# Twelve of the fourteen tiles that hold split weights made 64 bytes longer

## The chip, the cores and the metric

One core of a Trainium2 chip. The metric is the device time of one execution in microseconds (us).

## The reference

Top-32 attention over 4 batches, 8 heads, 576 positions and 64 columns a head, then two gated feed-forward layers (512 to 1536 to 512) over the 2304 tokens.

```python
scores = scale * np.matmul(q, k.transpose(0, 1, 3, 2))
kth = np.partition(scores, -top_k, axis=-1)[..., -top_k:-top_k + 1]
scores = np.where(scores >= kth, scores, -1000000000.0)
attn = np.exp(scores - np.max(scores, axis=-1, keepdims=True))
attn = attn / (np.sum(attn, axis=-1, keepdims=True) + 1e-09)
x = np.matmul(attn, v)                      # heads side by side: [2304, 512]
g = x @ w_gate
x = (g * (1.0 / (1.0 + np.exp(-g))) * (x @ w_val)) @ w_out        # moe
gate = 1.0 / (1.0 + np.exp(-(x @ w_gate2)))
return (gate * (x @ w_val2)) @ w_out2                             # moe2
```

## The kernel before

The 2304 tokens are cut into five chunks of 256, 512, 512, 512 and 512 tokens (`SIZES`, in units of 64). For each chunk `attention` makes the scores on TensorE, finds the 32nd largest of each row on VectorE (`top_full`, L888 and L890), normalizes and multiplies with v (`pv`, L977); then `moe` runs both feed-forward layers (L1018). The order of all instructions on all engines is written out beforehand by a planner (`Plan.run`), from durations that stand in the source. It knows nothing of addresses in the on-chip memory (SBUF), so the order is the same for any placement of the tiles.

Chunk 0 (mode "N") multiplies in plain fp32: `decode` unpacks a slab of 512 weight columns into a tile `wf` (GpSimd and ScalarE, L540 to L573), a DMA copies it to DRAM (`sw`, L576), and TensorE uses the tile at once as the stationary operand. The 72 tiles of chunk 0 go round a ring of 24 places: 12 in `home_pool` (`home0` to `home11`) and 12 in a pool of their own (`xf12` to `xf23`). So the first layer's gate and value slabs use home0 to home11 and then xf12 to xf23, its output slabs (input `hn`) home0 to home11, and the second layer's output slabs xf12 to xf23.

Chunks 1 to 4 (mode "P") split each operand into a high and a low part that are both fp32r. `slab` loads a slab again from DRAM into `raw`; `split_ops` makes the high part w[0] by a copy (ScalarE or GpSimd, L520 or L522) and the low part w[1] by a subtraction on GpSimd (L525). Seven pairs of tiles are used in turn (`w_tiles`): the pairs (home0, home1) to (home10, home11), and (wu0, wu1) in the pool `arena`. For one output tile, `mms` issues 12 matmuls of 128x512: four with w[0] and the inputs' high part, four with w[1] and the high part, four with w[0] and the low part. Inputs are `xh` and `xl` (pool `xs`), and `hh` and `hl`. Each matmul is preceded by its own weight load (LDWEIGHTS), which runs while the matmul before it streams its input. The scores of chunks 2 to 4 are fp32r too (`stacked_scores`, L678): stationary `qs`, inputs `kh` and `kl`, 288 columns.

Where the tiles lie follows from the order of the pools and the sizes of their tiles. In bytes from the start of a partition, before the change:

| tiles | start | bytes each |
|---|---|---|
| home0 to home11 (w[0], w[1] of six pairs; wf) | 17024 | 2048 |
| arena: wr0, wr1, wu0, wr2, wu1, wu2 | 41600 | 4096 or 2048 |
| a tile of 64 bytes, then xh, xl | 60096, 68288 | 8192 |
| eight (128 bytes), a tile of 64 bytes, x32, ... | 76480 | |
| hh, hl of chunks 1 to 4 | 159424, 184000 | 24576 |
| in chunk 0: xn0, xn1, hn | 159424, 163520, 167616 | 4096, 12288 |
| in chunk 0: xf12 to xf23 | 198336 | 2048 |
| qs | 212672 | 4096 |
| kh0, kh1, kl0, kl1 | 219072, 221376, 223680, 225984 | 2304 |

A slab's four blocks of 128x128 lie 512 bytes apart in its tile, the four inputs that meet them 2048 bytes apart (1024 in chunk 0). In this document the *lead* of a weight load is the address that it starts at, less the address at which the input of the matmul then running starts, modulo 512; with steps of 512, 1024 and 2048 it is the same for all blocks of a tile.

Of the kernel before, what the change touches and what calls it, by code (L numbers as in the profile page):

```python
# [19 lines left out]
P = 128  # L20
# [94 lines left out]
class Ring:  # L115
    def __init__(self, make, bufs):
        self.make, self.bufs, self.gens, self.next, self.after = make, bufs, [], 0, []
        self.before = lambda i: []
# [4 lines left out]

    def last(self, slot):
        return [g for g in self.gens if g.i % self.bufs == slot][-1:]


class Gen:
# [5 lines left out]
    def __getitem__(self, k):  # L134
        return self.tile[k]
# [212 lines left out]
def attn_moe_kernel(ctx: ExitStack, tc, qT, kT, qD, kD, vL, wall, outT):  # L348
# [6 lines left out]
    def pool(name, bufs, space=None):  # L355
        kw = {"space": space} if space is not None else {}
        return ctx.enter_context(tc.tile_pool(name=name, bufs=bufs, **kw))
# [19 lines left out]
    def phase_pool(n, name, bufs):  # L377
        if phases["now"] != n:
            if phases["stack"] is not None:
                phases["stack"].close()  # L380
            phases["now"], phases["stack"], phases["pools"] = n, ExitStack(), {}
            for nm, b in phase_rings[n]:
                phases["pools"][nm] = phases["stack"].enter_context(tc.tile_pool(name=f"{nm}{n}", bufs=b))
        return phases["pools"][name]
# [7 lines left out]
    home_pool = pool("home", 1)  # L392
# [9 lines left out]
    def home(nm, dtype=F32):  # L402
        i = int(nm.split("_")[1]) % (WF + XF if dtype == F32 else WF)
        if i >= WF:
            return phase_pool(0, "xf", XF).tile([P, 512], dtype, tag=f"xf{i}", name=nm, bufs=1)
        return home_pool.tile([P, 512], dtype, tag=f"home{i}", name=nm, bufs=1)
    R = {
        "x32": ring("x32", [P, NPAIR, TP], F32, 1),
        "sil": ring("sil", [P, HW], F32, SIL),
# [22 lines left out]
    kinds = [{"N": 0}.get(m, 1) for m in MODES]  # L432
    PHASE = [sorted(set(kinds)).index(k) for k in kinds]
    R["wf", 0] = Ring(home, WF + XF)
    phase_rings = {}
    for n in sorted(set(PHASE)):
# [3 lines left out]
        if "N" in kinds:  # L440
            T = max(SIZES[c] for c in mine if MODES[c] == "N") * 64
            specs.update(xn=([P, ND, T], F32, 2), hn=([P, NF, T], F32, 1), q=([P, S], F32, Q_RING),
                         k=([P, S], F32, K_RING))
# [35 lines left out]
    def w_tiles(nm):  # L479
        out = []  # L480
        for k in range(2):
            kind, i = w_home[2 * (int(nm.split("_")[1]) % WH) + k]
            out.append(home(f"w_{i}_{nm}", F32R) if kind == "wf" else
                       arena.tile([P, 512], F32R, tag=f"wu{i}", name=f"w_{i}_{nm}", bufs=1))
        return out
# [345 lines left out]
    def row_tile(sg, stg, a, e, pg):  # L831
        eg = new("e")

        def src():
            return sg[:, e].rearrange("p a b -> p (a b)")
        last, m0 = top_full(sg, src, stg, a)

        def base(eng):
# [26 lines left out]
        def norm(eng):  # L865
# [3 lines left out]
            else:  # L869
                nc.gpsimd.tensor_scalar(o, o, stg[:, 35:36], 1.0, op0=ALU.mult, op1=ALU.mult)  # L870
        x = op("act", act(S), drop, deps=[last], uses=[sg, stg], allocs=[eg], prio=P_EX[now[0]], table="exp")
        y = op(BASE, 0, base, deps=[last, m0], uses=[stg])
        y = op("act", 765, ex, deps=[x, y], uses=[eg, stg], allocs=[pg], prio=P_EX[now[0]], table="exp")
        y = op(EPS, 0, eps, deps=[y], uses=[stg])
# [122 lines left out]
    def moe(c):  # L997
# [16 lines left out]
        def mms(pg, blk, src, n, first, last):  # L1014
            i = 0
            for a, x in terms:
                for d in range(4):
                    nc.tensor.matmul(pg[:, :n], blk(a, d), src(x, d), start=first and i == 0,  # L1018
                                     stop=last and i == 4 * len(terms) - 1)
                    i += 1  # L1020
# [180 lines left out]
```

## Time and profile before

| | us |
|---|---|
| median of 3 runs | 1221.41 (1220.84 to 1222.0) |
| the profiled execution | 1221.71 |
| its span, first to last instruction | 1219.9 |

| engine | busy us | share of the span |
|---|---|---|
| TensorE, matmuls (PE) | 1165.9 | 96% |
| TensorE, weight loads (PEld) | 905.5 | 74% |
| GpSimd (POOL) | 945.3 | 77% |
| VectorE (DVE) | 868.8 | 71% |
| ScalarE (ACT) | 855.7 | 70% |

A matmul's record covers its way through the array, so records of neighbours overlap; how often matmuls follow each other is read from their starts. "L1018" is a line of the kernel before. The granted clock of TensorE is given as a share of 2.4 GHz.

### The profile page before, as it was taken

The page shows a single profiled execution, that of the slowest core. Times are in us where ns is not written, and L with a number is a line of the kernel's source. Part 1 is how long each engine was busy: PE and PEld are TensorE (multiplying, and loading weights), DVE is VectorE, ACT ScalarE, POOL GpSimd, SP SyncE. Part 2 cuts the span into 40 slices and gives each one's busy share as a digit, 9 for nine tenths or more (in the row PEclk, how much of TensorE's full clock was granted, in tenths as well). Part 3 has the DMA queues.
Part 4 walks back from the last instruction along what each step waited for, and adds up shares of the span by engine and source line. Part 5 has one row for each costly group of instructions (what it writes and reads, how often), then busy time and mean ns, then how long its engine had stood idle before and what let it go on. Part 6 is the DMA issues. An engine that isn't in the chain of part 4 may idle for free. (4 is left out here: it accounts for less than half of the span.)

```text
span 1219.9 us, 18873 instructions
## 1 busy us (share of the span) xinstructions
PE 1165.9 (96%) x6148; PEld 905.5 (74%) x6148; DVE 868.8 (71%) x1852; ACT 855.7 (70%) x1756; POOL 945.3 (77%) x954
## 2 busy tenths in 40 slices
PE   4698999998999999999899999999999999999998
PEld 1377866775777777878688787788777888888886
DVE  7999999999999999849498999999911101211110
ACT  6898999999886878858677978888733433432441
POOL 5677889896899798978777898879956786765761
PEclk9899999999999999999899999999999999999999
DMA  8787888883787886866647687667773333232320
GB/s 272 244 297 235 270 283 268 263 275 119 187 248 206 227 223 186 224 210 180 170 115 213 173 270 195 203 175 222 202 211 87 96 112 119 89 104 87 104 87 35
DMA packets 175170, 228.22 MB, mean 187 GB/s; under 512 B 112352, under 2 KB 117728, under 8 KB 175072
## 3 DMA queue, kind: packets, MB, share of 16 engines
q1 hardware_dynamic: 175072, 227.02, 62.6%
q8 instruction: 48, 0.79, 0.3%
q14 instruction: 50, 0.41, 0.1%
HBM read 149.13 MB, written 51.90 MB: 165 GB/s over the span
## 5 line engine op out<-in xcount | busy, mean ns | idle before, releaser
L525 POOL TENSOR_TENSOR w_w<-raw,w_w 128x512 fp32r<-128x512 f32 x288 | 374.7, 1307 | 116.6 <-ACT w_w L520 110.8
L1018 PE MATMUL ps_m<-xh,w_w 128*128 128x512 f32 x1536 | 385.0, 393 | 1.1 <-POOL xh L522 1.1
L1018 PEld LDWEIGHTS ps_m<-xh,w_w 128*128 128x128 f32 x1536 | 284.2, 188 | 61.3 <-POOL xh L522 1.5
L888 DVE MAX8 st<-wk 128x8 f32<-128x576 f32 x432 | 312.9, 745 | 0.4
L520 ACT ACTIVATE w_w<-raw 128x512 fp32r<-128x512 f32 x214 | 132.9, 624 | 124.1 <-PE ps_m L1018 71.0
L890 DVE MATCH_REPLACE8 wk<-st,wk 128x576 f32<-128x576 f32 x288 | 212.8, 740 | 0.0
L1018 PE MATMUL ps_m<-xl,w_w 128*128 128x512 f32 x768 | 207.3, 392 | 0.0
L1018 PE MATMUL ps_m<-hh,w_w 128*128 128x512 f32 x768 | 192.2, 392 | 0.0
L1018 PEld LDWEIGHTS ps_m<-xl,w_w 128*128 128x128 f32 x768 | 144.3, 188 | 31.7
L1018 PEld LDWEIGHTS ps_m<-hh,w_w 128*128 128x128 f32 x768 | 142.8, 188 | 30.8 <-issue 0.7
L525 POOL TENSOR_TENSOR hl<-h,hh 128x512 fp32r<-128x512 f32 x96 | 125.5, 1307 | 3.4 <-ACT hh L520 2.0
L888 DVE MAX8 st<-s 128x8 f32<-128x576 f32 x144 | 106.3, 745 | 24.8 <-ACT s L705 15.1
L848 ACT ACTIVATE e<-s,st 128x576 f32<-128x576 f32 x144 | 110.5, 769 | 15.9 <-DVE st L888 15.7
L989 DVE SCALAR_TENSOR_TENSOR h<-sil,ps_m 128x512 f32<-128x512 f32 x48 | 32.6, 680 | 117.1 <-PE ps_m L1018 117.1
L852 ACT ACTIVATE p<-e,st 128x576 f32<-128x576 f32 x144 | 110.7, 769 | 3.9 <-POOL pl L956 1.4
L1053 ACT ACTIVATE sil<-ps_m 128x512 f32<-128x512 f32 (+2 forms) x132 | 67.6, 512 | 58.1 <-PE ps_m L1018 57.8
L890 DVE MATCH_REPLACE8 wk<-st,s 128x576 f32<-128x576 f32 x144 | 106.5, 740 | 0.0
L1018 PE MATMUL ps_m<-hl,w_w 128*128 128x512 f32 x384 | 103.6, 392 | 0.0
L1018 PE MATMUL ps_m<-xn,wf 128*128 128x128 f32 (+1 forms) x576 | 93.9, 313 | 2.7 <-ACT xn L983 1.9
L977 PE MATMUL ps_v<-pt,v 128*64 128x128 f32 (+6 forms) x800 | 92.7, 377 | 0.2 <-ACT pt L936 0.2
L1018 PEld LDWEIGHTS ps_m<-xn,wf 128*128 128x128 f32 x576 | 80.3, 191 | 14.9 <-issue 3.9
L989 DVE SCALAR_TENSOR_TENSOR sil<-sil,ps_m 128x512 f32<-128x512 f32 (+1 forms) x72 | 39.0, 542 | 69.6 <-ACT sil L1053 69.6
(69 smaller groups left out, 1690.7 us busy)
## 6 DMA issues: line engine op xcount, KB each, us to landing
raw<-sw SPq DMA_DIRECT2D x144, 512.0 KB, 3.7
wr<-in_wall_dram SPq DMA_DIRECT2D x72, 512.0 KB, 4.7
sp_pl<-pl SPq DMA_DIRECT2D x44, 576.0 KB, 3.7
sw<-wf SPq DMA_DIRECT2D x72, 256.0 KB, 3.0
v<-in_vL_dram SPq DMA_DIRECT2D x34, 320.0 KB, 3.9
kr<-in_kD_dram SPq DMA_DIRECT2D x34, 288.0 KB, 3.1
k<-in_kT_dram SPq DMA_DIRECT2D x16, 288.0 KB, 4.5
out_dram<-h SPq DMA_DIRECT2D x16, 256.0 KB, 2.4
```

Of the source, the lines that this page charges most:

```text
L520: nc.scalar.activation(out=hi(), in_=raw(), func=AF.Copy)
L525: (nc.gpsimd if eng == "pool" else nc.vector).tensor_sub(lo(), (lo_raw or raw)(), lo_hi() if lo_hi else f32(hi()))
L848: nc.scalar.activation(out=eg[:], in_=src(), func=AF.Prelu, bias=stg[:, 31:32], scale=-1.0, alpha=1.0 / STEEP)
L852: nc.scalar.activation(out=pg[:, e * S:(e + 1) * S], in_=eg[:], func=AF.Exp, bias=stg[:, 32:33], scale=-STEEP, accum_out=stg[:, 33:34])
L888: nc.vector.max(out=stg[:, 4 * k:4 * k + 8], in_=src() if k == 0 else fresh[:])
L890: nc.vector.match_replace(out=fresh[:], in_to_replace=stg[:, 4 * k - 4:4 * k + 4], in_values=src() if k == 1 else fresh[:], imm_value=NEG)
L977: nc.tensor.matmul(og[64 * h:64 * h + 64, :W], vg[:, 8 + h if i == 4 else 4 * h + i], ptg[:, 4 if i == 4 else 5 * h + i, :W], start=(i == ...
L989: nc.vector.scalar_tensor_tensor(out=out, in0=t, scalar=1.0, in1=x, op0=ALU.add, op1=ALU.mult)
L1018: nc.tensor.matmul(pg[:, :n], blk(a, d), src(x, d), start=first and i == 0, stop=last and i == 4 * len(terms) - 1)
L1053: nc.scalar.activation(out=sg[:, :n], in_=pg[:, :n], func=AF.Tanh, scale=0.5)
```

## The change

Each of the twelve tiles in `home_pool` is asked for with 528 columns instead of 512, so it takes 2112 bytes instead of 2048. A small class `Front` hands out the first 512 columns of it, whatever is asked for. The two tiles wu0 and wu1 and the twelve tiles xf12 to xf23 stay as they are.

```diff
+class Front:
+    def __init__(self, t):
+        self.t, self.shape = t, [P, 512]
+
+    def __getitem__(self, k):
+        return self.t[:, :512]
+
...
         if i >= WF:
             return phase_pool(0, "xf", XF).tile([P, 512], dtype, tag=f"xf{i}", name=nm, bufs=1)
-        return home_pool.tile([P, 512], dtype, tag=f"home{i}", name=nm, bufs=1)
+        return Front(home_pool.tile([P, 528], dtype, tag=f"home{i}", name=nm, bufs=1))
```

Tile home(i) then starts at 17024 + 2112 i, and all tiles behind the home pool start 12 x 64 = 768 bytes later.

## Rows read from the trace of the kernel before

**Rows 1.** The chain that ended last, its shares by line

```profile
by line: PE ps_m L1018 33.2%; DVE st L888 4.5%; DVE wk L890 3.8%; PE ps_v L977 1.3%; PE ps_s L678 0.6%; DVE h L989 0.5%; issue 0.4%; ACT p L852 0.2%; POOL w_w L525 0.2%; ACT w_w L520 0.1%; ACT p L868 0.1%; DVE st L863 0.1%; ACT e L848 0.1%;
```

**Rows 2.** The same chain from 860 us: start us, us, what

```profile
899.70 16.69 PE ps_m L1018 x72
916.38 2.31 PE ps_v L977 x20
918.69 297.15 PE ps_m L1018 x1296
1215.85 0.03 ACTq L1124
1215.87 0.04 issue
1215.92 0.60 ACT h L1124
```

**Rows 3.** Stretches: busy us (instructions) of each engine, granted clock, DMA share, GB/s

```profile
400.00:500.00 100.00, 98.96 (x494) 78.53 (x493) 99.08 (x213) 82.20 (x163) 87.25 (x89) 1.00 0.81 214
700.00:800.00 100.00, 98.93 (x492) 77.42 (x492) 99.25 (x217) 83.20 (x170) 85.45 (x88) 1.00 0.75 220
800.00:905.00 105.00, 105.00 (x521) 82.94 (x520) 88.40 (x189) 76.92 (x142) 90.64 (x97) 1.00 0.74 207
918.69:1215.84 297.15, 297.14 (x1297) 243.17 (x1296) 35.77 (x52) 104.78 (x175) 190.38 (x155) 1.00 0.30 92
```

**Rows 4.** Instructions of L1018: duration ns min/median/max, first and last start

```profile
L1018 PEld LDWEIGHTS ps_m<-xh,w_w x1536: 186/188/192, 295.4 to 1181.3; 128*128 128x128 f32 x192
L1018 PE MATMUL ps_m<-xh,w_w x1536: 387/392/505, 295.4 to 1181.6; 128*128 128x512 f32 x192
...
L1018 PEld LDWEIGHTS ps_m<-hl,w_w x384: 187/188/189, 379.5 to 1215.2; 128*128 128x128 f32 x192
L1018 PE MATMUL ps_m<-hl,w_w x384: 388/392/398, 379.7 to 1215.4; 128*128 128x512 f32 x192
...
L1018 PE MATMUL ps_m<-hn,wf x192: 379/379/483, 140.9 to 279.0; 128*128 128x256 f32 x192
```

**Rows 5.** Order of time on PE, 818 to 827 us: start us, us, instructions

```profile
819.42 0.29 PE L678 MATMUL ps_s<-kh,qs 128*128 128x288 f32 x1
819.55 0.29 PE L678 MATMUL ps_s<-kl,qs 128*128 128x288 f32 x1
819.68 0.29 PE L678 MATMUL ps_s<-kh,qs 128*128 128x288 f32 x1
819.81 0.30 PE L678 MATMUL ps_s<-kl,qs 128*128 128x288 f32 x1
819.95 2.00 PE L1018 MATMUL ps_m<-xh,w_w 128*128 128x512 f32 x8
...
825.46 0.30 PE L678 MATMUL ps_s<-kh,qs 128*128 128x288 f32 x1
825.59 0.29 PE L678 MATMUL ps_s<-kl,qs 128*128 128x288 f32 x1
825.73 0.29 PE L678 MATMUL ps_s<-kh,qs 128*128 128x288 f32 x1
825.86 0.30 PE L678 MATMUL ps_s<-kl,qs 128*128 128x288 f32 x1
825.99 1.31 PE L1018 MATMUL ps_m<-xh,w_w 128*128 128x512 f32 x5
```

**Rows 6.** Instructions of L678, duration ns min/median/max, first and last start

```profile
L678 PEld LDWEIGHTS ps_s<-kh,qs x176: 186/188/192, 305.0 to 858.6; 128*128 128x128 f32 x176
L678 PEld LDWEIGHTS ps_s<-kl,qs x176: 186/188/192, 305.2 to 858.7; 128*128 128x128 f32 x176
```

**Rows 7.** Order of time on PE in chunk 0, around 146 and 259 us

```profile
145.82 5.34 PE L1018 MATMUL ps_m<-hn,wf 128*128 128x256 f32 x24
...
258.74 1.89 PE L1018 MATMUL ps_m<-hn,wf 128*128 128x256 f32 x8
```

**Rows 8.** Instructions on other engines that touch weight tiles: duration ns min/median/max

```profile
L525 POOL TENSOR_TENSOR w_w<-raw,w_w x288: 1266/1302/1812, 268.6 to 1197.3; 128x512 fp32r<-128x512 f32 x144
L525 POOL TENSOR_TENSOR hl<-h,hh x96: 1272/1302/1820, 307.3 to 1184.9; 128x512 fp32r<-128x512 f32 x96
L520 ACT ACTIVATE w_w<-raw x214: 612/624/635, 265.9 to 1196.6; 128x512 fp32r<-128x512 f32 x107
L520 ACT ACTIVATE hh<-h x82: 614/632/637, 312.4 to 1183.7; 128x512 fp32r<-128x512 f32 x82
L573 POOL TENSOR_TENSOR wf<-wf,wu x45: 1263/1277/1287, 12.8 to 266.1; 128x512 int32<-128x512 int32 x45
```

**Rows 9.** Stores of wf: DMA issues of 60 to 85, then 85 to 110 us

```profile
sw<-wf SPq DMA_DIRECT2D x6, 256.0 KB, 2.3
...
sw<-wf SPq DMA_DIRECT2D x5, 256.0 KB, 2.9
```

## The prediction

> **What bounds the kernel now.** I read the chain that ended last first. A third of the span on it is the feed-forward matmul, L1018, and some 8% the search for the 32nd largest score on VectorE [rows 1]. Its last link says most: from 918.69 us on, 1296 matmuls of L1018 follow each other without a gap, and 0.7 us behind them the kernel ends [rows 2]. Next, the stretches [rows 3]: in the last one PE is busy for 297.14 of 297.15 us, while ACT has 104.78 and POOL 190.38. In the three stretches shown between 400 and 905 us PE is busy for 98.9 to 100% and DVE for 84 to 99%, so there both set the pace. The granted clock is 1.00 in all four stretches, the level of 2.4 GHz, so no clock is to be won.
>
> So one number carries the case: how often an fp32r matmul of 512 columns starts. 297.15 us / 1296 = 229.3 ns. L1018 issues 3456 of them (1536 + 768 + 768 + 384, over the four inputs; [rows 4] has the first and the last group). A change of 1 ns in that number is worth 3456 x 1 ns = 3.5 us where PE is the limit throughout. What I have to judge is whether it hangs on where the weights lie relative to the input that streams while they are loaded.
>
> **The change part by part.** *What moves.* No instruction, semaphore or transfer is added, removed or reordered; the planner doesn't see addresses. Before, every split weight tile starts at 128 modulo 512, and xh, xl, hh and hl at 192, so every weight load of L1018 in chunks 1 to 4 has lead 448. After, the inputs move by 768 bytes, that is 256 modulo 512, and home(i) by 64 i: its lead becomes 448 - 256 + 64 i = 192 + 64 i modulo 512. The high parts (even i) get 192, 320, 448, 64, 192, 320, the low parts (odd i) 256, 384, 0, 128, 256, 384; the pair in wu0 and wu1 stays at 448. A high part serves 8 of 12 matmuls. So 5/7 x 2/3 + 6/7 x 1/3 = 16/21 of the matmuls, 2633 of 3456, get a new lead.
>
> *What a new lead costs a matmul.* The trace of before has no L1018 load in fp32r at another lead, but its nearest relatives have. (1) The score matmuls L678 are fp32r with 288 columns, and their groups of four come in two patterns. With the addresses of qs, kh and kl, the group at 819.42 has leads 256, 256, 0 and, where its last matmul runs beside the load of the next split weight, 448. The group at 825.46 has 128, 128, 384 and 320. From the first start to the start of the L1018 matmul behind them both take 0.53 us, 132.5 ns a matmul [rows 5]. So six of the eight multiples of 64 stand in these two groups, and 448, the lead of today, costs there what the five others do. (2) The weight load itself takes 186 to 192 ns, median 188, under all these leads: in L1018 at 448 [rows 4] and in L678 at the others [rows 6]. (3) In chunk 0, plain fp32, the first layer's hn matmuls take their weights from home tiles (lead 448) and the second layer's from xf tiles (lead 0). 24 of the one take 5.34 us, 8 of the other 1.89 us [rows 7]. Less the 0.379 us of the last one's own record [rows 4], that is 4.961 / 23 = 215.7 ns and 1.511 / 7 = 215.9 ns from start to start. No difference either; the home tiles' new leads in chunk 0 cost nothing by it.
>
> I take 0 for the term. Its bounds: the rows of (1) are given to 0.01 us, so a difference of up to 0.01 us over four matmuls, 2.5 ns each, could hide in one pair of groups; over some fifty such groups I allow 1.5 ns either way. 2633 x 1.5 ns = 3.9 us, in either direction, as a gain can't be excluded.
>
> *Other engines.* GpSimd's subtraction for the low part reads raw and w[0] and writes w[1]; before, all lie at the same place modulo 512. The same operation for hl has its three tiles at 384, 192 and 192, and the median of both is 1302 ns [rows 8]: 0. ScalarE's copy takes 624 ns for w[0] and 632 for hh [rows 8], so bounds of 0 and 8 ns x 214 copies = 1.7 us; I take 0 on the end, because PE hides it: in the last stretch ACT is idle for 192 us of 297 [rows 3]. If that cover were gone, it would cost at most those 1.7 us. In chunk 0, L573 writes home and xf tiles, at 128 and at 192 modulo 512, within 1263 to 1287 ns for all 45 [rows 8]: 0. The stores of wf land 2.3 us after issue in the stretch with home tiles and 2.9 us in that with xf tiles [rows 9], bounds of -0.6 and +0.6 us a store; what they wrote is loaded again only in chunk 1, so nothing waits for them: 0. If loads did wait for the last stores, it would be one such delay, 0.6 us.
>
> *The sum.* The profiled execution took 1221.71 us: 1219.9 of span and 1.8 around it. It lies 0.3 us above the median of 1221.41. All terms are 0, so the span stays 1219.9, the profiled execution 1221.7 and the median 1221.4.
>
> *A rule against this.* The trace shows 229.3 ns from start to start [rows 2]. The Trainium skill, in "TensorE: Matmul & The Clock Gate", section "Wait — 56ns, not 53.3ns?", gives back-to-back matmuls as the columns divided by 2.4 GHz plus about 2.5 ns, which would be 215.7 ns here; that is an estimate from the page, and the trace doesn't agree, it is 13.6 ns slower. The same page, section "Step-by-step: what each phase is for", says that TensorE reads moving operand and weights through two independent ports, so that a load takes no bandwidth from the running matmul. By that the 13.6 ns aren't a clash of the two reads, and no placement wins them back; the equal spacing in [rows 5] agrees.
>
> **The rivals.** *Faster: the distance above the plain rate is a clash that lead 448 has and others haven't.* The nearest row for an undisturbed rate is chunk 0's 215.7 ns for a pass over 256 columns of fp32 [rows 7], if an fp32r pass takes 512 columns in that time; then 229.3 - 215.7 = 13.6 ns are the clash. Freed for all 2633 matmuls: 2633 x 13.6 ns = 36 us, to about 1185; freed for half of them, about 1203. That is the most, since DVE sets the pace too before 905 us [rows 3]. For it: all matmuls of L1018 in fp32r share one lead today, so the trace can't show them without a clash. The plain rate on the Trainium skill's page "TensorE: Matmul & The Clock Gate" would give the same time. Against it: 448 and five other leads cost the same in the groups of four [rows 5]. Chance 0.08.
>
> *Slower: a clash at leads 64 or 192.* These two are nowhere in the trace with a load beside a matmul of L1018 or L678. They fall on home6 (64), home0 and home8 (192), three of seven high parts: 3/7 x 2/3 = 2/7 of the matmuls, 987. If a clash cost as much as the 13.6 ns above, that is 13.4 us, 1234.8 us. It passes 0.2% (2.44 us) from 2.5 ns a matmul. For it: nothing measured at these two. Against: the six others are alike, and 320 and 448 are odd multiples of 64 as well. Chance 0.08.
>
> *The change doesn't do what it says.* Should the pool round tiles up to multiples of 512 bytes, leads would not spread and the time would be that of before, 1221.4. The same time as the forecast, so no chance of its own is taken from it.
>
> **How the numbers follow.** Forecast 1221.4 us, no change that can be measured: 0.84 including the bounds of 3.9 us. A measurement of this kernel can tell about 0.2%, 2.4 us, from no change, and part of the bounds lies beyond that: I give 0.02 of the 0.84 to faster and 0.02 to slower. ScalarE's possible 1.7 us adds 0.01 to slower. With 0.08 for each rival: faster 0.10, same 0.79, slower 0.11. Range: 1221.4 - 3.9 = 1217.5 below; above, 3.9 + 1.7 us, 1227.0. It leaves out nearly all of the two rivals, 0.16.
>
> **What would show it.** The 1296 matmuls at the end should again take 297 us (229.3 ns each). With the rivals: down to 284 us (16/21 of 1296 x 13.6 ns = 13.4 us less), or up to 302 us (2/7 of 1296 x 13.6 ns = 5.0 us more), and then with a pattern by tile: slower runs of matmuls with home0, home6 and home8, and as fast as before with wu0. The weight loads' median should stay 188 ns, GpSimd's subtraction 1302 ns. I would be wrong if fp32r loads beside 512 columns behave otherwise than beside 288, if the address modulo 512 isn't what matters, or if the 768 bytes by which everything else moves touch a tile that was well placed by absolute address.

## The result, and the profile after

| | before | after |
|---|---|---|
| median of 18 runs each, us | 1221.25 (1217.43 to 1223.62) | 1227.76 (1222.63 to 1232.09) |
| profiled execution, us | 1221.71 | 1224.54 |
| its span, us | 1219.9 | 1222.7 |

The ratio is 1.0056, 95% interval 1.0045 to 1.0068: slower by 0.56%, 6.5 us between the medians. The forecast of no measurable change was wrong, and 1227.76 lies above its range. All lines of the kernel behind the new class stand 8 lines further down: L1018 is now L1026, L678 is L686, L525 is L533.

The end of the chain that ended last, after the change (start us, us, what):

```profile
914.38 2.31 PE ps_v L985 x20
916.69 301.96 PE ps_m L1026 x1296
1218.66 0.03 ACTq L1132
1218.68 0.04 issue
1218.73 0.60 ACT h L1132
```

The 1296 matmuls that took 297.15 us [rows 2] take 301.96 us, 233.0 ns each and not 229.3. That is 4.81 us in one stretch, with nothing else in the chain. The stretches of after (busy us and instructions of PE, weight loads, DVE, ACT and POOL, granted clock, DMA share, GB/s):

```profile
600.00:700.00 100.00, 99.14 (x506) 78.14 (x504) 88.01 (x183) 79.08 (x169) 78.21 (x81) 1.00 0.63 176
700.00:800.00 100.00, 99.36 (x494) 77.38 (x493) 99.90 (x222) 80.58 (x166) 84.17 (x87) 1.00 0.74 217
916.69:1218.65 301.96, 301.95 (x1297) 243.82 (x1296) 35.78 (x52) 104.80 (x175) 189.85 (x155) 1.00 0.29 90
```

In the last stretch the clock is 1.00, the level of 2.4 GHz, as before; ACT and POOL have as much work as before [rows 3], and as much idle time. So neither the clock nor a late weight tile explains it. The order of time on PE, inside that stretch, after the change:

```profile
1000.49 2.02 PE L1026 MATMUL ps_m<-hh,w_w 128*128 128x512 f32 x8
1002.35 1.10 PE L1026 MATMUL ps_m<-hl,w_w 128*128 128x512 f32 x4
1003.28 2.02 PE L1026 MATMUL ps_m<-hh,w_w 128*128 128x512 f32 x8
```

and before it:

```profile
1001.14 1.99 PE L1018 MATMUL ps_m<-hh,w_w 128*128 128x512 f32 x8
1002.98 1.08 PE L1018 MATMUL ps_m<-hl,w_w 128*128 128x512 f32 x4
1003.89 1.99 PE L1018 MATMUL ps_m<-hh,w_w 128*128 128x512 f32 x8
```

A group of twelve takes 2.79 us from start to start (1000.49 to 1003.28), where it took 2.75. No instruction and no wait lies between; the same matmuls simply follow each other more slowly. The weight loads' records don't tell: they are as long as before [rows 4].

```profile
L1026 PEld LDWEIGHTS ps_m<-xh,w_w x1536: 186/188/192, 294.9 to 1183.6; 128*128 128x128 f32 x192
L1026 PE MATMUL ps_m<-xh,w_w x1536: 387/394/505, 294.9 to 1183.8; 128*128 128x512 f32 x192
```

The matmuls' records are 394 ns in the median, up from 392. From the starts of the single matmuls between 295 and 905 us, the mean step between two of L1018 with nothing else between them (steps over 300 ns, which hold waits, left out) is 229.5 ns before and 231.4 ns after. For the 2160 matmuls ahead of the last 1296 that is up to 4.1 us more, less what DVE's own pace hides there. With the end's 4.8 us it makes 8.9 us; the medians differ by 6.5.

The two profiled executions differ by less, 2.8 us. One reason can be the clock. Between 599 and 605.5 us the granted clock of before was 0.50, 1.2 GHz, behind 3 us in which PE was busy for 0.82 us; after has 1.00 in that place. First two rows before the change, then one after:

```profile
596.00:599.00 3.00, 0.82 (x4) 0.35 (x2) 0.17 (x1) 2.98 (x10) 1.22 (x2) 0.96 0.39 147
...
599.00:605.50 6.50, 5.54 (x17) 2.34 (x19) 0.69 (x1) 1.90 (x4) 5.35 (x5) 0.50 0.41 126
```

```profile
599.00:605.50 6.50, 5.83 (x32) 2.98 (x33) 0.69 (x1) 2.73 (x6) 5.13 (x4) 1.00 0.47 147
```

That is 17 PE instructions against 32 in the same 6.5 us, so the dip costs about half of its length, some 3 us (an estimate). Such dips differ from trace to trace: that of the kernel with lead 0, below, has two of them, near 284 and 601 us, that of lead 320 one, near 285 us. The last 1296 matmuls have none in any trace, so the experiments are read from them first.

### The profile page after: what moved, and what is told of

Same layout as the page of the kernel before. It is cut to its first block, busy times and chain, and to the rows that moved or that the text cites. A ratio compares the mean times of both kernels' runs of the same rounds, so it can differ in the third digit from the quotient of the medians.

```text
span 1222.7 us, 18873 instructions
## 1 busy us (share of the span) xinstructions
PE 1172.1 (96%) x6148; PEld 906.5 (74%) x6148; DVE 869.7 (71%) x1852; ACT 856.0 (70%) x1756; POOL 945.3 (77%) x954
## 4 chain that ended last, share of the span: by engine, by line
PE 62%; DVE 24%; ACT 7%; POOL 3%; issue 2%; DMA 2%; SPq 0%; POOLq 0%; ACTq 0%; DVEq 0%
PE ps_m L1026 54%; DVE st L896 11%; DVE wk L898 9%; PE ps_v L985 4%; PE ps_s L686 3%; ACT p L860 1%; ACT wu L562 1%; ACT e L856 1%; DVE wf L578 1%; DMA wr<-in_wall_dram 1%; ACT pt L944 1%; PE ps_s L703 1%; ACT s L713 1%; ACT s L720 1%; ACT wf L548 1%
## 5 line engine op out<-in xcount | busy, mean ns | idle before, releaser
L533 POOL TENSOR_TENSOR w_w<-raw,w_w 128x512 fp32r<-128x512 f32 x288 | 375.2, 1309 | 119.5 <-ACT w_w L528 114.0
L1026 PE MATMUL ps_m<-xh,w_w 128*128 128x512 f32 x1536 | 388.3, 395 | 1.1 <-POOL xh L530 1.1
L1026 PEld LDWEIGHTS ps_m<-xh,w_w 128*128 128x128 f32 x1536 | 284.7, 188 | 63.8 <-POOL xh L530 1.5
L1026 PE MATMUL ps_m<-xl,w_w 128*128 128x512 f32 x768 | 209.6, 395 | 0.0
L1026 PE MATMUL ps_m<-hh,w_w 128*128 128x512 f32 x768 | 194.0, 395 | 0.0
L1026 PEld LDWEIGHTS ps_m<-xl,w_w 128*128 128x128 f32 x768 | 144.3, 188 | 34.0
L1026 PEld LDWEIGHTS ps_m<-hh,w_w 128*128 128x128 f32 x768 | 143.0, 188 | 32.3 <-issue 0.7
L533 POOL TENSOR_TENSOR hl<-h,hh 128x512 fp32r<-128x512 f32 x96 | 124.9, 1301 | 2.6 <-ACT hh L528 1.9
L1026 PE MATMUL ps_m<-hl,w_w 128*128 128x512 f32 x384 | 104.9, 395 | 0.0
L1026 PE MATMUL ps_m<-xn,wf 128*128 128x128 f32 (+1 forms) x576 | 93.6, 313 | 2.4 <-ACT xn L991 1.7
L1026 PEld LDWEIGHTS ps_m<-xn,wf 128*128 128x128 f32 x576 | 80.2, 191 | 14.3 <-issue 3.5
```

The lines of the kernel that those rows point to most:

```text
L533: (nc.gpsimd if eng == "pool" else nc.vector).tensor_sub(lo(), (lo_raw or raw)(), lo_hi() if lo_hi else f32(hi()))
```

## The experiments

The open question was which property of the new placement slows the matmuls. The theories: P, the absolute place of the inputs (all tiles behind the home pool moved by 768 bytes); M, that the lead differs from load to load; L, later called R, that each lead has a rate of its own. Leads are meant as in the section on the kernel before. Line numbers of L1018 differ by up to 8 where an edit adds or removes lines.

### All tiles moved, one lead

```diff
+    pool("pad0", 1).tile([P, 192], F32, tag="pad0", name="pad0")
     home_pool = pool("home", 1)
```

> A tile of 768 bytes is put ahead of the home pool, and all twelve home tiles keep 2048 bytes: every tile of the kernel lies where the changed kernel has it or 768 bytes later than before, and all split weights keep lead 448. Theory P (absolute place of the inputs, 192 to 448 modulo 512): as the changed kernel, about 1228 us, and the last 1296 matmuls take 302 us (233 ns each). Theory L (each lead has its own rate) and theory M (what costs is that the lead differs from load to load): as before, 1221 us, 297 us for the last 1296 (229.3 ns each).

Measured: 1220.68 us, ratio 1.0004 (0.999 to 1.0017). Its chain:

```profile
914.92 297.14 PE ps_m L1019 x1296
```

The end is that of before to 0.01 us, with xh, xl, hh and hl where the changed kernel has them. P, as stated, falls. The weights moved along, and 768 is three times 256, so this run alone can't exclude that the inputs' own place modulo 256 sets the rate; the pairs kernel below does.

### One other lead for all weights

Lead 0:

```diff
-    pool("pad", 1).tile([P, PAD], F32, tag="pad", name="pad")
```

> The 64-byte tile ahead of xh and xl is left out: all split weights at one lead, 0, instead of 448. Theory M: one lead for all is as before, 1221 us, 229 ns a matmul at the end. Theory L, with the rates that the changed kernel shows (230.5 ns at leads 0 and 256, 233 at the others): 230.5 ns a matmul, 1.3 ns x 3456 = 4 us more, about 1225 us. A larger effect, in either direction, would speak for L too.

Lead 384:

```diff
-PAD = 16
+PAD = 32
```

> The tile ahead of xh and xl is 128 bytes instead of 64: all split weights at lead 384. Theory M: as before, 1221 us, 229 ns a matmul at the end. Theory L, with the changed kernel's 233 ns at lead 384: 3.7 ns x 3456 = 13 us where PE is the limit throughout, 1226 to 1234 us, and 302 us for the last 1296.

Lead 320:

```diff
-PAD = 16
+PAD = 48
```

> The tile ahead of xh and xl is 192 bytes instead of 64: all split weights at lead 320. Theory M: as before, 1221 us, 229 ns a matmul at the end. Theory L, with the changed kernel's 233 ns at lead 320: 1226 to 1234 us, and 302 us for the last 1296.

Measured: lead 0: 1218.67 us, ratio 0.9989 (0.9976 to 1.0003). Lead 384: 1229.05 us, 1.0072 (1.0055 to 1.009). Lead 320: 1230.2 us, 1.0084 (1.0066 to 1.0101). The chains at the end, one fence for each of the three in this order:

```profile
919.94 196.75 PE ps_m L1017 x867
1116.69 0.01 issue
1116.70 97.55 PE ps_m L1017 x429
```

```profile
921.45 301.64 PE ps_m L1018 x1296
```

```profile
920.83 302.87 PE ps_m L1018 x1296
```

The same 1296 matmuls take 294.3, 301.6 or 302.9 us with nothing but the tile ahead of xh and xl changed. M as stated falls: one lead for all is not enough to be fast. L holds, and more strongly than the changed kernel had shown: at one lead a matmul takes anything from 227.1 ns (lead 0) to 233.7 ns (lead 320). For lead 0 the number expected under L missed, 230.5 ns and a slower kernel.

### The period

Lead 256 and lead 192 for all:

```diff
-PAD = 16
+PAD = 64
```

> The tile ahead of xh and xl is 256 bytes: all split weights at lead 256. Theory R (a constant lead lets the stream of matmuls settle at a rate of its own, and the rate repeats every 256 bytes): as lead 0, 226.7 ns a matmul at the end, 294 us for the last 1296, and 1218 to 1221 us in all. If the rate repeats only every 512 bytes, 256 is a value of its own, anywhere from 226 to 234 ns.

```diff
-PAD = 16
+PAD = 80
```

> The tile ahead of xh and xl is 320 bytes: all split weights at lead 192. Theory R with a period of 256: as lead 448, 228.9 ns a matmul at the end, 297 us for the last 1296, 1221 us in all. Without that period: another value, 226 to 234 ns.

Measured: lead 256: 1217.22 us, 0.9965 (0.9952 to 0.9979), faster than before. Lead 192: 1221.19 us, 1.0002 (0.9988 to 1.0017). First the chain at lead 256, then at 192:

```profile
918.24 196.75 PE ps_m L1018 x867
1114.99 0.01 issue
1115.00 97.55 PE ps_m L1018 x429
```

```profile
918.82 297.15 PE ps_m L1018 x1296
```

256 is as 0 and 192 as 448, both to 0.01 us: among multiples of 64 the rate repeats every 256 bytes. Lead 256 has the lowest time of all kernels that ran. Lead 0 has the same rate at the end, but its ratio came out 0.24% higher (0.9989 against 0.9965); the two intervals touch, the two ran on different chips, and whether the difference is real is open.

### Half a block of 64 bytes

```diff
-PAD = 16
+PAD = 8
```

> The tile ahead of xh and xl is 32 bytes instead of 64: all split weights at lead 480, half way between 448 (228.9 ns settled) and 0 (226.7 ns). If the rate follows the lead smoothly: 227.8 ns, 295.5 us for the last 1296, 1219 us in all. If only the 64-byte block in which the lead lies counts, it takes the value of 448 (297.2 us) or that of 0 (294.3 us). If half a block is a case of its own, any other value; below 294.3 us it would make the fastest placement.

Measured: 1232.01 us, 1.008 (1.0063 to 1.0097).

```profile
924.13 302.87 PE ps_m L1018 x1296
```

Lead 480 lies between 448 (297.15 us) and 0 (294.3 us) and is as slow as 320. The rate doesn't follow the lead smoothly, and 64 bytes are not the finest step that counts. In this kernel alone the inputs start at an odd multiple of 32 bytes; whether that or the lead makes it slow isn't shown.

The rates found, from the last 1296 matmuls:

| lead of all weights | last 1296, us | one, ns |
|---|---|---|
| 0, 256 | 294.3 | 227.1 |
| 192, 448 | 297.15 | 229.3 |
| 384 | 301.6 | 232.7 |
| 320, 480 | 302.9 | 233.7 |

These are means over the whole stretch. The expectations' 226.7, 228.9, 232.4 and 233.3 ns are those of its steady part and lie some 0.4 ns lower. Leads 64 and 128 never stood alone; by the period they would be as 320 and 384, and in the pairs kernel below they are.

### Mixed leads

Theory A says that a load costs what its lead costs when it is constant, whatever came before. With the table, the changed kernel's mix would take 2/3 x (4 x 297.15 + 3 x 302.87) / 7 for the high parts and 1/3 x (3 x 294.3 + 3 x 301.64 + 297.15) / 7 for the low parts: 299.0 us. It takes 301.96. So the slow leads explain 1.9 of the 4.8 us, and mixing costs 2.9 us on top. Four kernels look at that.

Both halves of a pair at one lead, seven leads in turn (with the class `Front` of the change):

```diff
+        return Front(home_pool.tile([P, 512 + 16 * (i % 2)], dtype, tag=f"home{i}", name=nm, bufs=1))
```

> Of the home tiles only those with odd numbers are 64 bytes longer: both halves of a pair keep one lead, and the seven pairs have 64, 128, 192, 256, 320, 384 and 448, so the lead changes every twelve matmuls and not every four. Theory A (each load costs what its lead costs when it is constant, whatever came before): the mean of the settled rates, with a period of 256, is (2 x 233.3 + 2 x 232.4 + 2 x 228.9 + 226.7) / 7 = 230.8 ns, 299 us for the last 1296, some 1225 us. Theory S (each change of lead throws the stream back to about 232 ns, from which it needs about ten matmuls to settle): 231.5 to 233 ns, 300 to 302 us, 1226 to 1229 us.

One pair of seven at another lead:

```diff
+    pool("pad", 1).tile([P, PAD], F32, tag="pad", name="pad")
     arena = pool("arena", 1)
-    pool("pad", 1).tile([P, PAD], F32, tag="pad", name="pad")
```

> The 64-byte tile lies ahead of the arena instead of behind it: the six home pairs keep lead 448, the pair in wu0 and wu1 gets lead 0. Theory A: one pair in seven goes from 228.9 to 226.7 ns, the mean is 228.6 ns, 296 us for the last 1296, 1220 to 1221 us. Theory S: the twelve matmuls of that pair and about ten behind it are unsettled at 230 to 232 ns, which makes the mean 229.3 to 229.8 ns, 297 to 298 us, 1221 to 1223 us; matmul by matmul, the pattern 232, 226, 229 of the other pairs is broken there and comes back some ten matmuls later.

High parts and low parts at different leads, first without a slow lead, then with one:

```diff
     home_pool = pool("home", 1)
+    pool("padx", 1).tile([P, 16], F32, tag="padx", name="padx")
+    home_odd = pool("homeo", 1)
...
-    pool("pad", 1).tile([P, PAD], F32, tag="pad", name="pad")
...
+        return (home_odd if i % 2 else home_pool).tile([P, 512], dtype, tag=f"home{i}", name=nm, bufs=1)
```

> The even home tiles lie together, then 64 bytes, then the odd ones, and no tile lies ahead of xh and xl: all high parts of the home pairs at lead 448, all low parts and the pair in wu0 and wu1 at lead 0. The lead changes every four matmuls, as in the changed kernel, but none of the slow leads 64, 128, 320 and 384 is left. Theory A (the mean of the settled rates): (6/7) x (2/3 x 228.9 + 1/3 x 226.7) + (1/7) x 226.7 = 227.9 ns, 295.4 us for the last 1296, 1218 to 1221 us. Theory F (four matmuls at a lead are too few, whichever leads): about 232 ns as in the changed kernel, 301 us, 1226 us. Theory B (the loads at 448 and 192 have two steady rates, 228.9 and 233.3 ns, and only a slow lead before them puts them on the slow one): as theory A.

```diff
     home_pool = pool("home", 1)
+    pool("padx", 1).tile([P, 32], F32, tag="padx", name="padx")
+    home_odd = pool("homeo", 1)
...
-PAD = 16
+PAD = 48
...
+        return (home_odd if i % 2 else home_pool).tile([P, 512], dtype, tag=f"home{i}", name=nm, bufs=1)
```

> The same with 128 bytes between even and odd home tiles and 192 bytes ahead of xh and xl: the high parts at lead 192, the low parts and the pair in wu0 and wu1 at the slow lead 320. Theory A: (6/7) x (2/3 x 228.9 + 1/3 x 233.3) + (1/7) x 233.3 = 230.8 ns, 299.1 us for the last 1296, 1224 to 1225 us. Theories B and F: the matmuls that load a high part stay at 233 ns too, 302 us for the last 1296, 1228 to 1230 us.

Measured, with theory A worked out from the table above:

| kernel | lead changes | last 1296, us | A, us | total, us | ratio |
|---|---|---|---|---|---|
| one pair of seven at 0 | twice in 84 matmuls | 296.75 | 296.7 | 1220.77 | 1.0005 (0.9985 to 1.0025) |
| pairs at seven leads | every 12 | 300.04 | 299.7 | 1225.37 | 1.0029 (1.0014 to 1.0043) |
| high 192, low 320 | every 4 | 300.38 | 299.6 | 1225.79 | 1.0035 (1.0023 to 1.0048) |
| high 448, low 0 | every 4 | 297.66 | 295.9 | 1221.17 | 1.0001 (0.9991 to 1.0011) |
| the change | every 4 | 301.96 | 299.0 | 1227.76 | 1.0056 (1.0045 to 1.0068) |

The chains of the one pair at 0, of the pairs, of high 192 with low 320, and of high 448 with low 0, a fence each:

```profile
919.98 198.38 PE ps_m L1018 x867
1118.36 0.00 issue
1118.36 98.37 PE ps_m L1018 x429
```

```profile
920.61 300.04 PE ps_m L1026 x1296
```

```profile
919.37 300.38 PE ps_m L1020 x1296
```

```profile
917.14 198.97 PE ps_m L1019 x867
1116.11 0.00 issue
1116.12 98.69 PE ps_m L1019 x429
```

Two groups of twelve from the one-pair kernel, in ns from start to start, near 1000 us: first the pair in wu0 and wu1 (lead 0), then home0 and home1 (448).

```
227 227 226 227 227 226 227 227 226 227 227 226
229 231 226 229 232 226 229 232 226 229 231 226
```

Theory S falls here: the first step behind the change of lead has the new lead's rate, and the mean is what A says. In the pairs kernel that isn't so at every change. Its pair at lead 256, which follows that at 192, near 1012 us, from the step that loads its first block on:

```
236 228 233 231 226 227 227 226 227 227 226 227
```

Four steps are unsettled, not ten. Behind the fourth, the pairs have the rates that their leads have alone (means of the groups between 1004 and 1117 us): 233.3 ns at 64 and 320, 232.4 at 128 and 384, 228.9 at 192 and 448, 226.7 at 256. So the lead sets the rate and not the inputs' own place: in this kernel the inputs lie at 64 modulo 256 throughout and the weights differ, in the kernels with one lead the weights lie at 128 modulo 256 and the inputs differ.

Theory A holds where twelve matmuls share a lead, to 0.4 us; in the pairs kernel some changes lose in the first four steps and some gain. Theory F as stated falls as well: high 448 with low 0 is far below 301 us. But four in a row are paid dearer than A says. A group of twelve from that kernel, home2 and home3, again near 1000 us:

```
232 226 229 | 231 236 228 233 | 230 226 229 232 | 226
```

The four steps between the first two bars, during which the low part's four blocks at lead 0 are loaded, average 232 ns and not the 227 that lead 0 has alone; this is the 1.7 us between 297.66 and 295.9. The same change ahead of this kernel's pair in wu0 and wu1 costs nothing. In the last stretches of the one-pair kernel, the pairs and this one, changes from 192 or 448 to 0 or 256 differ by the step just before them: behind one of 231 or 232 ns the next four average 226 to 227 ns (28 of 28 cases), behind one of 225 to 230 ns they average 232 (105 of 105; the first 40 matmuls and steps over 260 ns left out). No run set that step on its own, so it is a correlation. In the changed kernel even the pair in wu0 and wu1, twelve at lead 448, steps at 233, 234, 233 nearly throughout, while the same lead gives 226, 229, 232 where it is alone. So a run can stay on a slower pattern of the same lead. Theory B, that a slow lead ahead of them puts 448 and 192 there, is not borne out in general: beside lead 320 the loads at 192 average 230.3 ns, not 233. What decides in general which pattern a run takes is left open.

### Longer groups of score matmuls

The prediction rested on the groups of four of L678. Here each group is issued four times over:

```diff
-                for h in range(2):
+                for h in [0, 1] * 4:
```

> Each group of four score matmuls of chunks 2 to 4 is issued four times over, with the same result: sixteen matmuls of 288 columns in a row, those of the first half of the keys all at leads 0 or 256, those of the second half all at 128 or 384. Some 1056 matmuls of 132 ns more, so about 1221 + 139 = 1360 us at most. Theory C (288 columns feel the lead like 512, and four in a row are too few to show it): towards the end of the sixteen, the groups at 0 and 256 are 4 to 6 ns a matmul faster than those at 128 and 384. Theory N (288 columns don't feel it): both stay at 131 to 134 ns from the first to the last.

Measured: 1352.59 us, one run. The order of time on PE, the start of a group at leads 0 and 256 and the instruction behind it, then the same of a group at 128 and 384:

```profile
332.10 0.29 PE L678 MATMUL ps_s<-kh,qs 128*128 128x288 f32 x1
332.24 0.29 PE L678 MATMUL ps_s<-kl,qs 128*128 128x288 f32 x1
...
334.21 2.00 PE L1018 MATMUL ps_m<-xh,w_w 128*128 128x512 f32 x8
...
336.96 0.29 PE L678 MATMUL ps_s<-kh,qs 128*128 128x288 f32 x1
...
339.09 2.01 PE L1018 MATMUL ps_m<-xh,w_w 128*128 128x512 f32 x8
```

Sixteen matmuls take 2.11 us at the fast leads, 131.9 ns each, and 2.13 us at the slow ones, 133.1 ns. Over all 44 groups of each kind the mean steps are 131.6 and 133.4 ns (steps over 160 ns, which hold waits, left out), from the second matmul to the last without a trend. Theory C's 4 to 6 ns are not there, and neither is theory N's equality: 288 columns feel the lead, by 1 to 2 ns, where 512 columns feel it by 5.7 (294.3 against 301.64 us over 1296). The length of the group doesn't matter.

## Why the prediction was wrong

*What bounds the kernel: right.* The step from start to start of L1018's fp32r matmuls carried the case, 1 ns of it is 3.5 us at most, and the 4.8 us of the last stretch lie there whole.

*What moves: right.* The rates of the later kernels, pair by pair, fit leads worked out in the same way.

*What a new lead costs a matmul: the step that failed,* with its 0 and its bound of 1.5 ns. The rates differ by 6.6 ns (227.1 to 233.7), and the changed kernel's mix costs 3.7 ns on the mean of all matmuls in the last stretch, 4.9 ns for each with a new lead (4.81 us over 16/21 of 1296). Two things were mis-sized in that one term. Each lead has its own rate, which explains 1.9 of the 4.8 us. And a load was priced by its own lead alone, so there was no term for a lead that changes every four matmuls: the other 2.9 us. The first alone would be 5.0 us at most over all 3456 matmuls, 1226.4 us in all (an estimate from the table of rates), still inside the range.

- Evidence (1) failed, the score matmuls. It took a price for 288 columns as one for 512. The repeated groups show a difference of 1.2 ns a matmul at 288 columns, in two single groups; at the resolution of [rows 5], 2.5 ns, that doesn't show. Read over all 44 groups of each kind, the trace of before has it: 131.6 and 132.9 ns a step (steps over 160 ns left out). The bound of 1.5 ns was about right for what was measured and too small by a factor of three for what it was applied to (from 448 to 320 it is 4.4 ns). The text named this as a way to be wrong, but gave it no chance of its own and no room in the range.
- Besides, the two groups of [rows 5] mix leads that the later runs set apart: 256, 256, 0 and 448, all of them fast, against 128, 128, 384 and 320, all of them slow. They were the right comparison, in the wrong shape of matmul.
- Evidence (2) failed, the length of the weight loads. At leads 256 and 320, whose matmuls step at 227 and 234 ns, the loads' median is 188 ns all the same. At 256, then at 320:

```profile
L1018 PEld LDWEIGHTS ps_m<-xh,w_w x1536: 186/188/193, 295.4 to 1178.4; 128*128 128x128 f32 x192
L1018 PE MATMUL ps_m<-xh,w_w x1536: 387/389/501, 295.4 to 1178.6; 128*128 128x512 f32 x192
```

```profile
L1018 PEld LDWEIGHTS ps_m<-xh,w_w x1536: 186/188/194, 297.5 to 1188.5; 128*128 128x128 f32 x192
L1018 PE MATMUL ps_m<-xh,w_w x1536: 388/394/504, 297.5 to 1188.8; 128*128 128x512 f32 x192
```

  What is lost shows in the matmul's record, 389 and 394 ns, and in the starts.
- Evidence (3), plain fp32, was right for fp32 and says nothing on fp32r: in the changed kernel the hn matmuls of chunk 0 stand at all eight leads and step at 215.8 to 216.3 ns at each.

*Other engines: right.* In the last stretch POOL has 189.85 us and ACT 104.80, as before within 0.6 us. GpSimd's subtraction for w[1] keeps its median of 1302 ns, ScalarE's copy for w[0] takes 623.

*The rivals.* Slower came true, but not by the mechanism named. The rival put the clash at leads 64 and 192, because nothing had been measured there; 64 is slow, as it turned out, but 192 is as good as 448, and 320 and 384, which counted as measured, are among the bad ones. Nor did its pattern come: wu0 and wu1 step at 233 ns too. Its 5.0 us for the last stretch is close to the 4.8 measured by chance: it is made of 1.9 us for slow leads and 2.9 us for mixing. Faster was right in part: 448 is not the best lead, and another placement wins 2.2 ns a matmul, at leads 0 and 256, not 13.6. It takes one lead for all tiles, which this change doesn't give. That the rest of the 13.6 ns is a clash isn't shown.

*The rule weighed against it.* The two independent read ports of the Trainium skill ("TensorE: Matmul & The Clock Gate", section "Step-by-step: what each phase is for") were read as a reason against any such effect. For fp32r the runs contradict what was drawn from it, that no placement wins anything: the same two streams cost 227.1 to 233.7 ns a matmul, by the lead. Where rule and measurement differ, the measurement decides; whether the ports are independent the runs don't tell. The page's 215.7 ns (an estimate from its section "Wait — 56ns, not 53.3ns?") was reached at none of the leads tried.

*The chances.* 0.79 for no change rested on three pieces of evidence, none of which was the instruction, shape and type that the change touches.

## What to carry to other kernels

A price is safest from the very instruction, shape and type that the change touches; where the trace of before has that instruction at one setting only, it can't tell whether the setting matters, and the range has to say so. When fp32r matmuls bound a kernel, the place of the weight tile against the streamed input is worth a few runs with a small tile ahead of the inputs: here lead 256 in place of 448, one constant, gave 0.35% (ratio 0.9965), and lead 480 cost 0.8%. Keep the lead the same for all weight tiles; spreading them over all offsets gave the mean of good and bad placements here, and more on top.

## What the runs showed of the hardware that I had not expected

The time from one fp32r matmul of 512 columns to the next depends on the address of the weights that are being loaded, less that of the input that streams: 227.1 ns at 0 and 256 bytes, 229.3 at 192 and 448, 232.7 at 384, 233.7 at 320 and 480. Moving both by 768 bytes changes nothing (297.14 against 297.15 us), and the steady rates are the same whether the inputs or the weights are moved to reach a lead (226.7 ns at 256, 228.9 at 192 and 448, 232.4 at 384, 233.3 at 320). Plain fp32 at 256 columns doesn't feel it (215.8 to 216.3 ns), fp32r at 288 columns little (131.6 and 133.4 ns). What in the memory or the array causes it, the runs don't tell.

At one and the same lead there can be more than one steady pattern: 448 steps by 226, 229, 232 ns where it is alone and by 233, 233, 234 in the changed kernel. A change of lead after twelve matmuls costs at most 0.3 ns a matmul on average (300.04 against 299.7 us over 1296), one after four up to 2.3 ns (301.96 against 299.0 us). After a change from 192 or 448 to 0 or 256, the next four steps average 226 to 227 ns where the step before it was 231 or 232 ns, and 232 ns where it was 225 to 230; that is seen in the traces and not tested by a run of its own.
